# The row scatters of layer 0 set apart in a kernel of one scan and two expert layers

## The chip, the cores and the metric

The kernel runs on one core of a Trainium2 chip. The metric is the device time in microseconds (us) of one execution. The five engines have instruction streams of their own and meet at semaphores: TensorE (PE in the rows) multiplies, ScalarE (ACT) and VectorE (DVE) work on tiles and empty PSUM, GpSimd (POOL) does small elementwise work and issues the indirect DMAs, and SyncE (SP) issues the other DMAs. Each engine takes its own instructions strictly in order.

## What is computed

```python
for t in range(S):                         # gated scan, B = 2, S = 5056, D = 256
    h = f[:, t] * h + (1 - f[:, t]) * x[:, t];  y[:, t] = h
# then twice, on N = 10112 rows, E = 8 experts, F = 1024:
idx = argmax(logits, 1)                    # layer 0: normalised rows, layer 1: x @ w_gate
for e in range(E):
    mask = idx == e
    out[mask] = gate[mask, None] * (relu(x[mask] @ w1[e]) @ w2[e])
```

Each row goes through one expert per layer. The second layer routes the rows that the first one gives.

## The kernel before

**Rows and tables.** Rows are sorted by expert in DRAM. The table `X[0]` takes the rows of the scan, and `X[1]` takes the rows that layer 0 gives. A row holds two fp16 halves (high and low part), its scale and its token number, 1032 bytes in all. A tile is 128 rows of one expert, read back from the table by a transposing DMA (`t_load`, L755). A result row is written to its sorted place by an indirect DMA that GpSimd issues, the *row scatter*: `p_put` (L638, tile `row`) writes rows of the scan to `X[0]`, and the end of `m_slot` (L948, tile `trow`) writes rows of layer 0 to `X[1]`. Each scatter writes 128 rows.

**Steps.** The main loop goes through 332 executed *steps*. In a step TensorE does the first product of one tile and one half of the hidden columns (`mm1`, 24 matmuls, L780) into a PSUM tile `hps`. ScalarE and VectorE then empty it into `hT` (`evac`, L788 and L187), and TensorE does the second product of the step three before (`mm2`, 12 matmuls, L802; `lag` is 3). All other work is hung on the steps by a table of offsets and priorities, `(step offset, priority)`. Within a step, work is emitted by rising priority. `mm1` has 5, `evac` 50, `mm2` 55. On TensorE, ScalarE, GpSimd and SyncE the order is kept as emitted from step 17 on (`man`); on VectorE a scheduler sets it.

**Pairs.** Two tiles of layer 0 make a *pair*. When the second half of a tile is done, its row sums are copied to `osum`, and `m_sq` (L825, ScalarE) writes squares into a new `trow` buffer. Then come scaling (`m_scale`: VectorE's `pi`, `tsc`, `us`; GpSimd's `lf`, `COPY trow`, `inv`), logits, the choice of the expert (`m_top`, with GpSimd's `tsh`), the exponential, the gate weight (`m_gat`, with GpSimd's `trow<-tse,lf`) and the place in the table (`m_slot`). Before the change `m_slot` ends with the two scatters of the pair, back to back. There are five `trow` buffers (pool `rp`). Thus `m_sq` of the fifth pair after this one must wait until both of this pair's scatters have landed.

**Three groups of layer 0.** The first 4 tiles (group 1) and the last 21 (group 2, `swap`) run all their first halves and then all their second halves; the 58 between them (group 0) run both halves in turn, so that a pair ends every fourth step. In group 2, whose second halves run in steps 145 to 165, a pair ends every second step. I call its pairs P0 to P10, the last of one tile. P0's second tile leaves `mm2` in step 149, and each next pair two steps later. For group 2 the table `mg` puts `m_slot` nine steps on, so P0's scatters belong to step 158 before the change, P1's to step 160, and so on. P5's first `m_sq` stands in step 160 and needs P0's `trow` buffer; P6's stands in step 162 and needs P1's; P10's stands in step 170 and needs P5's. A step with two transposes of a pair needs six PSUM buffers in two steps, and pool `pb` has six, so in this stretch `hps` of a step takes the buffer that `hps` of two steps before gave back.

**Row groups of the scan** are four tiles; their scatters stand in four steps one after the other, at priority 12 (`put`), in a step's early part. In the middle of the program a period is eight steps long, with four scatters of `row` and four of `trow`.

Of the kernel before, what the change touches and what calls it, by code (L numbers as in the profile page):

```python
# [11 lines left out]
I32 = mybir.dt.int32  # L12
U32 = mybir.dt.uint32
ACTF = mybir.ActivationFunctionType
# [32 lines left out]
 'alias': 8,  # L47
 'mans': 17,
 'xtn': 48,
 'md': {'turn': (3, 58),  # L50
        'logits': (8, 3),
        'top': (8, 51),
# [2 lines left out]
        'rank': (10, 46),  # L55
        'slot': (11, 13),
        'up': (12, 45),
        'done': (12, 57)},
 'hiv': (2,),
 'y1': 'V',  # L60
 'wg': (0, 0, 0, 0),
# [63 lines left out]
def scan_moe_moe_kernel(ctx, tc, xf, emb, cst, tmp, w1a, w2a, w1b, w2b, out, seq, cfg=CFG):  # L125
# [6 lines left out]
    CT = 2  # L132
# [9 lines left out]
    BOUND = DUM + P - 1  # L142
# [3 lines left out]
    inside = [False]  # L146
# [30 lines left out]
    X = [dr.tile([DUM + P, RW // 2], I32, name=f"X{m}") for m in range(2)]  # L177
# [5 lines left out]
    V, A, G, T, SP = nc.vector, nc.scalar, nc.gpsimd, nc.tensor, nc.sync  # L183

    def stt(eng, out, in0, s, in1, op0, op1, **kw):
        assert eng is V
        return eng.scalar_tensor_tensor(out=out, in0=in0, scalar=s, in1=in1, op0=op0, op1=op1, **kw)  # L187
# [15 lines left out]
    def ins_of(i):  # L203
        return getattr(i, "ins", i)

    def x_write(m, i, group="Xw"):
        i = ins_of(i)
        tc.declare_no_dep(i, group=f"Xw{m}", reason="disjoint rows")
        tc.declare_no_dep(i, group=f"Xr{m}", reason="disjoint rows")
        if xpad[m]:  # L210
            tc.declare_no_dep(i, group=f"Xp{m}", reason="disjoint rows")
        tc.add_to_no_dep_group(f"{group}{m}", i)
        xw[m].append(i)
        if group == "Xp":
            xpad[m].append(i)
# [128 lines left out]
    now = [0]  # L344
# [288 lines left out]
    def p_put(q, rows):  # L633
        p = pq[q]
        for i in rows:
            if i >= p["g"]:
                return
            x_write(0, G.indirect_dma_start(out=X[0], out_offset=IndirectOffsetOnAxis(ap=p["sl"][:, i, 0:1], axis=0),  # L638
                                            in_=p["row"][:, i, :].bitcast(I32), in_offset=None, bounds_check=BOUND,
                                            oob_is_err=False))  # L640
            yield


# [69 lines left out]


    ring = {}

    wreg = [T.alloc_register(f"wa{i}") for i in range(16)]
    vreg = [T.alloc_register(f"va{i}") for i in range(4)]
# [65 lines left out]
    def evac(t, h):  # L784
        hps = t.pop("hps")
        hT = hp.tile([P, 8, P], F16, name="hT", tag="hT", bufs=LAG + 2)
        hh = hT.rearrange("p (a c) q -> p a (c q)", a=2)
        A.activation(out=hh[:, 0], in_=hps, func=ACTF.Relu)  # L788
        stt(V, hh[:, 1], hps, 0.0, hh[:, 0], ALU.max, ALU.subtract)
        t["hT", h] = hT  # L790

# [142 lines left out]
    def m_slot(d):  # L934
        g = len(d["t"])
        pz = d["er"]
        assert ranked[1] == 1
        ranked[1] = 0
        tt(V, pz, RK[:, G4:G4 + g], d["oh"][:, 0:g], ALU.mult)
        yield  # L940
        slf = sm.tile([P, CT, 1], F32, name="tslf", tag="tslf")[:, 0:g]
        V.tensor_reduce(out=slf, in_=pz, axis=AX.X, op=ALU.add)
        yield
        sl = sm.tile([P, CT, 1], I32, name="tsl", tag="tsl")[:, 0:g]
        stt(V, sl, slf, 1.0, d["inv"].unsqueeze(2), ALU.mult, ALU.add)
        yield
        for i in range(len(d["t"])):
            x_write(1, G.indirect_dma_start(out=X[1], out_offset=IndirectOffsetOnAxis(ap=sl[:, i, 0:1], axis=0),  # L948
                                            in_=d["row"][:, i].bitcast(I32), in_offset=None, bounds_check=BOUND,
                                            oob_is_err=False))  # L950
            yield

    def m_up(d):
        rank_up(1, d["oh"], CT)
# [26 lines left out]
    for m in range(2):  # L981
        done = 0
# [13 lines left out]
        for part in (tl, tails[m]):  # L996
            for j in range(0, len(part), CT):
                d = dict(t=part[j:j + CT], at=j)
# [25 lines left out]
    def at(s, prio, fn, *a):  # L1024
        seqn[0] += 1
        slots.setdefault(s, []).append((prio, seqn[0], fn, a))
# [26 lines left out]
    for c in range(NCH):  # L1053
        b = s0[c]
        PO = cfg["p"]

        def pa(name, fn, arg, b=b):
            if c < cfg["cps"][0] // CT and name in cfg["urgent"]:
                fn = first_of_all(fn)
            at(b + PO[name][0], PO[name][1], fn, arg)  # L1060

        if 2 <= c < cfg["alias"]:
            at(first - 2 + (c - 2) // 2, 2, p_load, c)
        elif c >= 2:
            pa("load", p_load, c)
        for name, fn in (("gate", p_gate), ("scan", p_scan), ("mm", p_mm), ("sq", p_sq), ("pow", p_pow), ("hi", p_hi), ("lo", p_lo)):
            pa(name, fn, c)
        if c % 2 or c == NCH - 1:
            q = c // 2
            for name, fn in (("norm", p_norm), ("top", p_top), ("rank", p_rank), ("rec", p_rec), ("exp", p_exp), ("slot", p_slot),  # L1070
                             ("up", p_up), ("gat", p_gat)):
                pa(name, fn, q)
            b, prio = s0[c] + PO["put"][0], PO["put"][1]
            if b < 0:
                at(b, prio, first_of_all(p_put) if c < cfg["cps"][0] // CT else p_put, q, range(G4))
            else:
                for j in range(G4):
                    at(b + j, prio, p_put, q, (j,))

            def cp0(q):  # L1080
                for m, cnt, n, fin, key in cpl:
                    if m == 0 and key not in xcnt and cnt <= min(NT, (q + 1) * G4):
                        checkpoint(m, n, fin, key, min(NT, (q + 1) * G4))

            pa("cp", cp0, q)
# [104 lines left out]
    def fin_unit(u, i):  # L1190
        t, h = units[u]
        if t["grp"] and h == 0:
            new_acc(t)
            at(i + 1, 10, o_partial, t)
        elif h == 1:
            if t["m"] == 1:
                at(i + 1, 10, s2, t)
                return
            MO = dict(cfg["m"], **cfg["mg"]) if t["grp"] else dict(cfg["m"], **cfg["md"]) if by_dma(t["pair"]) else cfg["m"]

            def ma(name, fn, arg):
                at(i + MO[name][0], MO[name][1], fn, arg)

            ma("sum", o_sum, t)
            ma("sq", m_sq, t)
            d = t["pair"]
            if t["pi"] == len(d["t"]) - 1:
                for name, fn in (("scale", m_scale), ("split", m_split), ("turn", m_turn), ("turn2", m_turn2),
                                 ("logits", m_logits), ("top", m_top), ("exp", m_exp), ("rank", m_rank),
                                 ("gat", m_gat), ("slot", m_slot), ("up", m_up), ("done", done_pair)):  # L1210
                    ma(name, fn, d)

    def drain(g):
        for _ in g or ():
            pass
# [8 lines left out]
    def last_tiles(m):  # L1224
        tl = tails[m]
        if not tl:
            return
        n = counts[m]
        inside[0] = True
        if m:  # L1230
            with tc.If(n > tl[0]["j"], label=f"tail{m}"):
                us = [(t, h) for t in tl for h in range(2)]
                for i in range(len(us) + 2):
                    if i < len(us):
                        t, h = us[i]
                        if h == 0:
                            t_load(t, 0)
                            t_reg(t)
                        mm1(t, h)
                        evac(t, h)  # L1240
                    if i >= 2:
                        t, h = us[i - 2]
                        mm2(t, h, h == 0, h == 1)
                        if h == 1:
                            drain(s2(t))
            return
        with tc.If(n > tl[0]["j"], label=f"tail{m}"):
            kept[0] = {}
            assert ranked[1] == 0
            for d in [t["pair"] for t in tl if t["pi"] == 0]:  # L1250
                for t in d["t"]:
                    t_load(t, 0, qp.tile([P, 8, TW], F16, name="xt8", tag="q")[:, 0:4, 0:P])
                    t_reg(t)
                    for h in range(2):
                        mm1(t, h)
                        evac(t, h)
                        mm2(t, h, h == 0, h == 1)
                    drain(o_sum(t))
                    m_sq(t)
                for fn in (m_scale, m_split, m_turn, m_turn2, m_logits, m_top, m_exp, m_rank, m_gat, m_slot, m_up):  # L1260
                    drain(fn(d))
                routed[0] += len(d["t"])
            kept[0] = None
        inside[0] = False
# [4 lines left out]
    with ExitStack() as region:  # L1269
# [5 lines left out]
        i = first - 2  # L1275
# [117 lines left out]
```

## Time and profile before

| | |
|---|---|
| median of 3 runs | 1064.48 us (1055.07, 1064.48, 1067.7) |
| the profiled execution's own time | 1052.77 us |
| its span, first to last instruction | 1050.9 us |
| granted TensorE clock, mean | 0.985 |
| TensorE busy | 996.1 us (95%) |
| VectorE, ScalarE, GpSimd busy | 602.3, 529.2, 407.8 us |
| software DMA queue (the scatters) | 31.51 MB, 11.7% of 16 engines |
| TensorE's slices (tenths of 40 equal slices) | 5557 in the first four, then 9 |

Read it from TensorE. After the first four slices, in which the scan starts and the first tiles are routed, it is nearly always busy. A later step can lengthen the time only where TensorE is made to wait, or give time back only where it waits now. In a timeline row the first number is the start in us, the second the busy time, and the brackets hold the idle time of that engine just before and what ended it.

### The profile page before, as it was taken

Reading aid. Unit: us, or ns where it says so; the run is one execution under the profiler, and the core shown is the slowest. Engines: PE = TensorE matmul, PEld = TensorE weight load, DVE = VectorE, ACT = ScalarE, POOL = GpSimd, SP = SyncE. Lnnn points to the kernel's source line nnn. Section 1 sums busy time; section 2 is a strip of 40 time slices with the busy share of each in tenths; the row PEclk is TensorE's granted clock in tenths of the full one; section 3 lists DMA queues with packets and bytes.
Section 4 is the critical chain, followed back from the end, with each engine's and each line's share of the span. In section 5 each row is a group of like instructions: output and inputs, shape, how many; then the busy total and the mean of one; then the engine's idle time right before and its main releaser. Section 6 shows DMA issues by size and latency. Waiting matters only on the chain. (4 is left out here: it accounts for less than half of the span.)

```text
span 1050.9 us, 36737 instructions
## 1 busy us (share of the span) xinstructions
PE 996.1 (95%) x13267; PEld 932.6 (89%) x13267; DVE 602.3 (57%) x1927; ACT 529.2 (50%) x1301; POOL 407.8 (39%) x666
## 2 busy tenths in 40 slices
PE   5557999999999999999999999999999999999997
PEld 4436889999999999999998999999999999999997
DVE  7988877787778777665449778443222222222221
ACT  6978555665655565665346466443333333333332
POOL 5834645666666565332002550243222222222222
PEclk9967999999999999999999999999999999999999
DMA  9798436777677673875479699653322222222220
GB/s 352 244 342 209 132 59 120 144 136 130 124 127 127 152 125 94 195 196 149 62 170 205 123 197 267 117 103 72 52 52 53 52 53 48 45 50 44 47 51 31
DMA packets 195612, 132.69 MB, mean 126 GB/s; under 512 B 169601, under 2 KB 172558, under 8 KB 195440
## 3 DMA queue, kind: packets, MB, share of 16 engines
q1 hardware_dynamic: 172384, 60.18, 29.7%
q10 hardware_dynamic: 11200, 38.62, 14.7%
q0 software_dynamic: 11856, 31.51, 11.7%
q8 instruction: 118, 1.93, 0.8%
q14 instruction: 54, 0.44, 0.2%
HBM read 58.89 MB, written 38.85 MB: 93 GB/s over the span
## 5 line engine op out<-in xcount | busy, mean ns | idle before, releaser
L780 PE MATMUL hps<-xT,W 128*128 128x128 f16 x7968 | 504.9, 220 | 6.9 <-DVE hT L187 3.1
L802 PE MATMUL ops<-W,hT 128*128 x3984 | 489.3, 272 | 1.6 <-ACT acc L806 0.9
L780 PEld LDWEIGHTS <-W 128*128 x7968 | 475.6, 98 | 16.0 <-issue 6.3
L187 DVE SCALAR_TENSOR_TENSOR hT<-hps,hT 128x512 f16<-128x512 f32 x332 | 228.6, 688 | 318.4 <-ACT hT L788 315.7
L802 PEld LDWEIGHTS <-hT 128*128 128x128 f16 x3984 | 374.3, 98 | 41.4 <-issue 2.0
L788 ACT ACTIVATE hT<-hps 128x512 f16<-128x512 f32 x332 | 198.0, 596 | 303.2 <-PE hps L780 284.0
L970 POOL DMA_INDIRECT out<-osum,ti x83 | 81.1, 977 | 291.4 <-ACT osum L966 189.5
L948 POOL DMA_INDIRECT X<-trow,tsl x83 | 97.1, 1170 | 53.2 <-DVE tsl L187 18.0
L638 POOL DMA_INDIRECT X<-row,sl x79 | 92.8, 1174 | 55.1 <-issue 37.7
L966 ACT ACTIVATE osum<-ops,exr 128x256 f32<-128x256 f32 x62 | 29.3, 473 | 47.0 <-PE ops L802 44.8
L195 POOL TENSOR_TENSOR lf<-exr,us 128x2 f32<-128x2 f32 (+1 forms) x42 | 9.7, 231 | 102.6 <-DMA W<-WD 44.0
L187 DVE SCALAR_TENSOR_TENSOR W<-ws,W 128x1024 f16<-128x1024 f32 x34 | 41.5, 1220 | 8.7 <-ACT W L373 8.7
L373 ACT ACTIVATE W<-ws 128x1024 f16<-128x1024 f32 x35 | 37.1, 1060 | 12.5 <-DMA ws<-w2b 8.6
L825 ACT ACTIVATE trow<-osum 128x256 f16<-128x256 f32 x83 | 34.9, 420 | 16.0 <-DMA X<-trow,tsl 7.6
L492 DVE TENSOR_TENSOR_SCAN xf<-xf 128x256 f32<-128x256 f32 (+3 forms) x64 | 42.8, 710 | 0.1
L507 PE MATMUL yt<-cs,xf 128*128 128x128 f32 x126 | 28.3, 303 | 15.2 <-DVE xf L492 10.2
L814 ACT ACTIVATE osum<-ops 128x256 f32<-128x256 f32 x58 | 22.2, 382 | 38.3 <-PE ops L802 38.3
L187 DVE SCALAR_TENSOR_TENSOR trow<-osum,tsc,trow 128x256 f16<-128x256 f32 x83 | 36.7, 481 | 4.1 <-ACT trow L840 3.2
L187 DVE SCALAR_TENSOR_TENSOR xf<-xf 128x512 f32<-128x512 f32 (+1 forms) x32 | 21.8, 681 | 26.7 <-POOL xf L192 19.9
L547 ACT ACTIVATE row<-yt,sc 128x256 f16<-128x256 f32 x79 | 33.5, 481 | 6.5 <-DVE sc L192 6.5
L840 ACT ACTIVATE trow<-osum,tsc 128x256 f16<-128x256 f32 x62 | 28.1, 500 | 16.5 <-DVE tsc L192 14.9
L187 DVE SCALAR_TENSOR_TENSOR row<-yt,sc,row 128x256 f16<-128x256 f32 x79 | 36.0, 472 | 0.2 <-ACT row L547 0.2
(149 smaller groups left out, 929.2 us busy)
## 6 DMA issues: line engine op xcount, KB each, us to landing
xf<-xf ACTq DMA_DIRECT2D x28, 512.0 KB
ws<-w1b ACTq DMA_DIRECT2D x16, 512.0 KB
ws<-w2b ACTq DMA_DIRECT2D x16, 512.0 KB
W<-w1a SPq DMA_DIRECT2D x11, 512.0 KB
W<-xf SPq DMA_DIRECT2D x8, 512.0 KB
ws<-w2a ACTq DMA_DIRECT2D x8, 512.0 KB
WD<-wq SPq DMA_DIRECT2D x8, 512.0 KB
W<-WD SPq DMA_DIRECT2D x8, 512.0 KB
```

Of the source, the lines that this page charges most:

```text
L187: return eng.scalar_tensor_tensor(out=out, in0=in0, scalar=s, in1=in1, op0=op0, op1=op1, **kw)
L373: A.activation(out=hi, in_=src, func=ACTF.Copy, scale=64.0)
L492: V.tensor_tensor_scan(out=t[:, k, lo:hi], data0=t[:, 2 + k, lo:hi], data1=t[:, k, lo:hi], initial=init, op0=ALU.mult, op1=ALU.subtract)
L547: A.activation(out=p["row"][:, o + i, 0:D], in_=yv(d["yt"][i]), func=ACTF.Copy, scale=p["sc"][:, o + i:o + i + 1])
L638: x_write(0, G.indirect_dma_start(out=X[0], out_offset=IndirectOffsetOnAxis(ap=p["sl"][:, i, 0:1], axis=0), in_=p["row"][:, i, :].bitcast( ...
L780: T.matmul(out=hps[:, c, :], lhsT=w, rhs=xt[:, a, :], start=(n == 0), stop=(n == 5))
L788: A.activation(out=hh[:, 0], in_=hps, func=ACTF.Relu)
L802: T.matmul(out=o, lhsT=hT[:, a + k, :], rhs=w[:, b * D:(b + 1) * D], start=(first and k == 0 and n == 0), stop=(last and k == 3 and n == 2))
L825: A.activation(out=d["row"][:, i, D:2 * D], in_=t["O"], func=ACTF.Square, scale=0.25, accum_out=d["ss"][:, i:i + 1])
L948: x_write(1, G.indirect_dma_start(out=X[1], out_offset=IndirectOffsetOnAxis(ap=sl[:, i, 0:1], axis=0), in_=d["row"][:, i].bitcast(I32), in ...
L966: A.activation(out=r, in_=o, func=ACTF.Copy, scale=ex0[:, 0:1])
L970: i = ins_of(G.indirect_dma_start(out=out, out_offset=IndirectOffsetOnAxis(ap=ti, axis=0), in_=r, in_offset=None, bounds_check=N - 1, oob_ ...
```

## The change

The two scatters of a pair leave `m_slot` and become two calls of a new function `m_put`. The first stands in the step in which `m_slot` ended before; the second stands two steps later in group 0 and one step later in groups 1 and 2 (`'apart': (2, 1)`). Their priority is 40 where `m_slot` has a low one (groups 1 and 2, and the pairs of group 0 that are turned by DMA), and 55 otherwise. From step 17 on the row scatters of the scan move from priority 12 to 54 of the same step (`'late'`). Every scatter after step 17 gets one more wait: for the last ScalarE `evac` that had been recorded when it was emitted. At priority 40 that is the `evac` of the step in front, at 54 and 55 that of its own step. `done` of the DMA-turned pairs, which counts routed tiles, moves from 12 to 13 steps. No instruction is added or removed.

```diff
+ 'apart': (2, 1),
+ 'late': 54,
...
-        'done': (12, 57)},
+        'done': (13, 57)},
...
-            x_write(0, G.indirect_dma_start(out=X[0], out_offset=IndirectOffsetOnAxis(ap=p["sl"][:, i, 0:1], axis=0),
+            x_write(0, paced(G.indirect_dma_start(out=X[0], out_offset=IndirectOffsetOnAxis(ap=p["sl"][:, i, 0:1], axis=0),
...
+    evs = []
+
+    def paced(i):
+        if now[0] > cfg["mans"] and not inside[0]:
+            tc.add_manual_dep(ins_of(i), evs[-1].name, mybir.DependencyInfo(mybir.DependencyClass.Sync, mybir.DependencyReason.DATA),
+                              reason="one step apart")
+        return i
...
-        A.activation(out=hh[:, 0], in_=hps, func=ACTF.Relu)
+        evs.append(ins_of(A.activation(out=hh[:, 0], in_=hps, func=ACTF.Relu)))
...
-        yield
-        for i in range(len(d["t"])):
-            x_write(1, G.indirect_dma_start(out=X[1], out_offset=IndirectOffsetOnAxis(ap=sl[:, i, 0:1], axis=0),
-                                            in_=d["row"][:, i].bitcast(I32), in_offset=None, bounds_check=BOUND,
-                                            oob_is_err=False))
-            yield
+        d["sl"] = sl
+
+    def m_put(d, i):
+        if i < len(d["t"]):
+            x_write(1, paced(G.indirect_dma_start(out=X[1], out_offset=IndirectOffsetOnAxis(ap=d["sl"][:, i, 0:1], axis=0),
...
-                    at(b + j, prio, p_put, q, (j,))
+                    at(b + j, prio if b < cfg["mans"] else cfg["late"], p_put, q, (j,))
...
+                for j in range(CT):
+                    at(i + MO["slot"][0] + cfg["apart"][bool(t["grp"])] * j, 40 if MO["slot"][1] < 40 else 55, m_put, d, j)
```

The order of instructions on TensorE, ScalarE and SyncE stays as it was. GpSimd's order changes in two ways. The first place is a period in the middle of the program (group 0). `X_100<-trow,tsl` is a scatter of a pair, `X_99<-row,sl` one of the scan's rows, `xf` a gate of the scan, `tsh` and `lf` small products of layer 0. Before:

```order
L192 TENSOR_SCALAR xf<-xf,fa,fb 128x256 x2
L948 DMA X_100<-trow,tsl 82048x258 x2
L638 DMA X_99<-row,sl 82048x258
L195 TENSOR_TENSOR tsh<-tsh,lf 128x16
L638 DMA X_99<-row,sl 82048x258
L195 TENSOR_TENSOR lf<-exr,us 128x2
```

and with the change, at the same place on GpSimd:

```order
L194 TENSOR_SCALAR xf<-xf,fa,fb 128x256 x2
L959 DMA X_100<-trow,tsl 82048x258
L640 DMA X_99<-row,sl 82048x258 x2
L197 TENSOR_TENSOR tsh<-tsh,lf 128x16
L959 DMA X_100<-trow,tsl 82048x258
L640 DMA X_99<-row,sl 82048x258
L197 TENSOR_TENSOR lf<-exr,us 128x2
```

The pair's second scatter has gone behind `tsh`, and one row scatter that stood ahead of the first rows shown now stands behind the pair's first scatter.

The second place is group 2, where a pair ends every second step. Before, on GpSimd, from the scaling of one pair (`lf`, `COPY`, `inv`) to the scatters of the pair four ahead of it:

```order
L195 TENSOR_TENSOR lf<-exr,us 128x2
L844 COPY trow<-exr 128x2
L192 TENSOR_SCALAR inv<-exr 128x2
L195 TENSOR_TENSOR tsh<-tsh,lf 128x16
L195 TENSOR_TENSOR trow<-tse,lf 128x2
L948 DMA X_100<-trow,tsl 82048x258 x2
```

and with the change, from the first scatter of one pair to the first of the next:

```order
L959 DMA X_100<-trow,tsl 82048x258
L197 TENSOR_TENSOR lf<-exr,us 128x2
L853 COPY trow<-exr 128x2
L194 TENSOR_SCALAR inv<-exr 128x2
L197 TENSOR_TENSOR tsh<-tsh,lf 128x16
L959 DMA X_100<-trow,tsl 82048x258
L197 TENSOR_TENSOR trow<-tse,lf 128x2
L959 DMA X_100<-trow,tsl 82048x258
```

The second scatter of a pair (the second DMA row) now stands behind `lf`, `COPY`, `inv` and `tsh` of the step after; `lf` belongs to the scaling of the pair four later. On VectorE some 25 small instructions around step 160 change places among themselves; elsewhere its order is the same but for two swaps of neighbours.

## Rows read from the trace of the kernel before

**Rows 1.** The page's 40 slices: tenths busy, for TensorE.

```profile
PE   5557999999999999999999999999999999999997
```

**Rows 2.** Busy time by stretch; the first line names the columns.

```profile
core 0: us, PE busy (x) PEld busy (x) DVE busy (x) ACT busy (x) POOL busy (x), PEclk, DMA share, GB/s
...
300.00:325.00 25.00, 25.00 (x352) 23.84 (x350) 20.34 (x88) 15.22 (x47) 15.96 (x27) 1.00 0.75 129
...
575.00:600.00 25.00, 22.79 (x334) 21.23 (x332) 18.91 (x91) 12.79 (x37) 12.32 (x27) 1.00 0.72 128
```

**Rows 3.** Waits of TensorE from 150 us on: us in total, times, longest.

```profile
PE hps L780 <- DVE osum L195: 1.9, 1, 1.9
```

**Rows 4.** GpSimd's timeline in group 0: start, busy, line, out<-in, idle before.

```profile
300.86 1.46 POOL L948 DMA_INDIRECT X<-trow,tsl  x1 [0.16 <-POOL xf L192]
302.63 1.23 POOL L948 DMA_INDIRECT X<-trow,tsl  x1 [0.31 <-issue]
304.16 0.97 POOL L638 DMA_INDIRECT X<-row,sl  x1 [0.30 <-issue]
...
306.10 1.01 POOL L638 DMA_INDIRECT X<-row,sl  x1 [0.51 <-issue]
308.37 0.18 POOL L195 TENSOR_TENSOR lf<-exr,us 128x2 f32<-128x2 f32 x1 [1.26 <-DVE tse L187]
```

**Rows 5.** ScalarE's timeline in the same stretch, two of the `evac`.

```profile
302.79 0.60 ACT L788 ACTIVATE hT<-hps 128x512 f16<-128x512 f32 x1 [1.13 <-PE hps L780]
...
305.49 0.60 ACT L788 ACTIVATE hT<-hps 128x512 f16<-128x512 f32 x1 [0.96 <-PE hps L780]
```

**Rows 6.** GpSimd's timeline in group 2, P0 to P5.

```profile
571.89 0.97 POOL L948 DMA_INDIRECT X<-trow,tsl  x1 [0.30 <-issue]
...
576.22 0.21 POOL L195 TENSOR_TENSOR tsh<-tsh,lf 128x16 f32<-128x16 f32 x1
...
578.87 1.51 POOL L948 DMA_INDIRECT X<-trow,tsl  x1 [0.30 <-issue]
584.69 0.37 POOL L195 TENSOR_TENSOR lf<-exr,us 128x2 f32<-128x2 f32 x1 [4.31 <-DVE tsh L187]
...
585.92 0.30 POOL L195 TENSOR_TENSOR tsh<-tsh,lf 128x16 f32<-128x16 f32 x1
...
589.42 0.97 POOL L948 DMA_INDIRECT X<-trow,tsl  x1 [0.30 <-issue]
...
605.83 0.97 POOL L948 DMA_INDIRECT X<-trow,tsl  x1 [0.30 <-issue]
```

**Rows 7.** ScalarE's timeline in group 2: first `m_sq` of P5, P6, P7, P10.

```profile
582.12 0.42 ACT L825 ACTIVATE trow<-osum 128x256 f16<-128x256 f32 x1 [3.84 <-DMA X<-trow,tsl]
...
587.20 0.42 ACT L825 ACTIVATE trow<-osum 128x256 f16<-128x256 f32 x1 [2.13 <-DVE toh L187]
...
593.83 0.42 ACT L825 ACTIVATE trow<-osum 128x256 f16<-128x256 f32 x1 [2.87 <-DMA X<-trow,tsl]
...
610.72 0.42 ACT L825 ACTIVATE trow<-osum 128x256 f16<-128x256 f32 x1 [0.94 <-DMA X<-trow,tsl]
```

**Rows 8.** TensorE's timeline: `mm1` of steps 162, 170 and 172.

```profile
584.36 1.50 PE L780 MATMUL hps<-xT,W 128*128 128x128 f16 x24
...
609.20 1.50 PE L780 MATMUL hps<-xT,W 128*128 128x128 f16 x24
...
615.25 1.50 PE L780 MATMUL hps<-xT,W 128*128 128x128 f16 x24
```

**Rows 9.** VectorE's timeline: its part of `evac` of steps 160 and 170.

```profile
583.14 0.69 DVE L187 SCALAR_TENSOR_TENSOR hT<-hps,hT 128x512 f16<-128x512 f32 x1 [2.92 <-ACT hT L788]
...
612.59 0.68 DVE L187 SCALAR_TENSOR_TENSOR hT<-hps,hT 128x512 f16<-128x512 f32 x1
```

**Rows 10.** Line L948, the pairs' scatters, over the run: from issue to landing.

```profile
DMA to landing us min/median/max: 2.6/4.6/6.1
```

More of the change, by code (lines that the diff above doesn't have):

```diff
@@ L637, in p_put @@
                 return
-            x_write(0, G.indirect_dma_start(out=X[0], out_offset=IndirectOffsetOnAxis(ap=p["sl"][:, i, 0:1], axis=0),
-                                            in_=p["row"][:, i, :].bitcast(I32), in_offset=None, bounds_check=BOUND,
-                                            oob_is_err=False))
+            x_write(0, paced(G.indirect_dma_start(out=X[0], out_offset=IndirectOffsetOnAxis(ap=p["sl"][:, i, 0:1], axis=0),
+                                                  in_=p["row"][:, i, :].bitcast(I32), in_offset=None, bounds_check=BOUND,
+                                                  oob_is_err=False)))
             yield
@@ L945, in m_slot @@
         stt(V, sl, slf, 1.0, d["inv"].unsqueeze(2), ALU.mult, ALU.add)
-        yield
-        for i in range(len(d["t"])):
-            x_write(1, G.indirect_dma_start(out=X[1], out_offset=IndirectOffsetOnAxis(ap=sl[:, i, 0:1], axis=0),
-                                            in_=d["row"][:, i].bitcast(I32), in_offset=None, bounds_check=BOUND,
-                                            oob_is_err=False))
-            yield
+        d["sl"] = sl
+    def m_put(d, i):
+        if i < len(d["t"]):
+            x_write(1, paced(G.indirect_dma_start(out=X[1], out_offset=IndirectOffsetOnAxis(ap=d["sl"][:, i, 0:1], axis=0),
+                                                  in_=d["row"][:, i].bitcast(I32), in_offset=None, bounds_check=BOUND,
+                                                  oob_is_err=False)))
     def m_up(d):
@@ L1261, in last_tiles @@
                     drain(fn(d))
+                for j in range(CT):
+                    m_put(d, j)
                 routed[0] += len(d["t"])
```

## Prediction

> **What bounds the kernel now.** I read the page's slices first, then the busy times by stretch, then TensorE's waits, then the timelines of GpSimd, ScalarE, VectorE and TensorE where the scatters stand.
>
> The slices show TensorE at nine tenths or more from the fifth slice on [rows 1]. The change acts from step 17 on, which lies behind the four slow slices, so it cannot touch the start. From 300 to 325 us TensorE is busy for all 25.00 us while GpSimd has work for 15.96 us [rows 2]. A scatter that lands sooner is worth nothing there, since nothing on TensorE waits for it. The one stretch with real idle time is 575 to 600 us, with 22.79 of 25 us busy [rows 2], and the longest wait of TensorE after 150 us lies in it: 1.9 us [rows 3]. That stretch is group 2, where pairs end every second step. So the question is what the change does to group 2, and whether it disturbs group 0.
>
> What the reader should see in group 2 is one chain. ScalarE's `m_sq` of P5 begins at 582.12 after 3.84 us of idle time that ended with the landing of a `trow` scatter [rows 7]. The buffer it needs is P0's, and P0's second scatter was issued at 571.89 [rows 6]. P7 waits 2.87 us in the same way for P2 (issue 589.42, start 593.83), and P10 waits 0.94 us for P5 (605.83, 610.72) [rows 6, 7]. The second scatter of a pair is thus already the last event ahead of ScalarE in this stretch, and everything later on ScalarE, `evac` above all, stands behind it. VectorE's `evac` of step 160 waits 2.92 us for ScalarE [rows 9], and `mm1` of step 162 starts at 584.36, 0.53 us after that `evac` ended (583.14 + 0.69) [rows 8, 9]. The buffers of the accumulator leave about half a microsecond between the two.
>
> **The change part by part.** *Row scatters at priority 54, and the waits in group 0.* Laid out from the rows: the pair's first scatter can start at 300.86 as now and ends at 302.3. Two row scatters follow. The first needs an `evac` that is over. The second needs the one that ends at 303.39 (302.79 + 0.60), and GpSimd comes to it at about 303.6. `tsh` follows, then the pair's second scatter, then a row scatter behind the `evac` that ends at 306.09, where GpSimd comes at about 307. With 1.0 us for that one, `lf` starts at about 308.4, and it starts at 308.37 now, after 1.26 us of idle time for a result of VectorE [rows 4, 5]. The new waits fall where GpSimd was not ready anyway, so I cost them at nothing. The cover is GpSimd's free time, 25 − 15.96 = 9.0 us in 25 [rows 2]; if each of the seven or so scatters of a period really waited 1.3 us, the cover would be gone. That is the fourth case below. What stands behind the waiting scatters on GpSimd is the gate of the scan, `ri`, `lf` and `tsh`; TensorE needs what comes of them steps later.
>
> *The second scatter two steps later in group 0.* The buffer is needed again by the fifth pair after it, 20 steps on, while the pair's scatters stand 8 to 13 steps after the pair. It costs nothing. `done` at 13 has the same answer: the checkpoint for layer 1 is set off by pairs whose offsets don't change.
>
> *The second scatter one step later in group 2.* Here the order on GpSimd counts. P0's second scatter now stands behind `lf`, `COPY`, `inv` and `tsh` of step 159. Today that `tsh` ends at 576.43 (576.22 + 0.21) [rows 6]. With the 0.30 us that stands ahead of a scatter [rows 6], the issue moves from 571.89 to about 576.7. When does it land? The nearest issue is P1's second at 578.87, for which P6 was released by 587.20, at most 8.3 us later [rows 6, 7]. With 8.3 us P5 is released at 585.0 rather than 582.12, 2.9 us late. The bounds are 582.1 (it lands no later than now, since other traffic held up the early issue) and 576.7 + 10.2 = 586.9 (the 571.89 to 582.12 of today).
>
> *And then a loop closes.* `lf` in front of P1's second scatter is the scaling of P5 and so needs P5's `m_sq`. P1's scatter now waits for P5, P6 waits for P1's scatter, P2's scatter waits for P6, and so on to P10. Before the change both scatters of P1 stood ahead of P5's scaling, so there was no such loop of two steps. Its length comes from rows of today. From `m_sq` of P5 (582.12) to the end of `tsh` (585.92 + 0.30 = 586.22) and 0.30 us to the issue is 4.4 us [rows 6, 7]. Then the scatter must land. The least on the page is 2.6 us and the middle 4.6 [rows 10]; P7's and P10's waits give 4.4 (589.42 to 593.83) and 4.9 (605.83 to 610.72) [rows 6, 7], but for the second of two scatters issued back to back, and the new one goes alone. I take 3.6, halfway from 2.6 to 4.6, with 2.6 and 4.9 as bounds. The loop is then 8.0 us (7.0 to 9.3), while TensorE needs 6.05 for the same two steps (609.20 to 615.25) [rows 8].
>
> *The sum.* There are five loops from P5 to P10. P10's `m_sq` would start at 585.0 + 5 × 8.0 = 625.0 and not at 610.72 [rows 7], 14.3 us late. TensorE can take up some of it: `mm1` of step 172 starts 2.0 us after the `evac` of step 170 has ended (615.25 against 612.59 + 0.68) [rows 8, 9]. It loses 14.3 − 2.0 = 12.3 us. With the low bounds it is 582.1 + 35.0 = 617.1, so 6.4 − 2.0 = 4.4 us; with the high ones 586.9 + 46.5 = 633.4, so 20.7 us. After step 172 the pairs are over and TensorE sets the pace again, with nothing given back. Against the profiled execution's own 1052.77 us the sum is 1065.
>
> For the landing there is a rule to weigh. The rows have waits of 4.4 and 4.9 us and a least of 2.6 [rows 6, 7, 10]. The Trainium skill, "DMA: Bandwidth & Descriptors", section "Anatomy of one DMA — SWDGE (gpsimd) path", gives a transfer issued by GpSimd a fixed 2.0 us and its bytes at 436 GB/s. As an estimate from that page, 132 KB would take 2.3 us, the loop 6.7, and the loss would be 5.8 rather than 12.3 us. No row has a landing that short, so the measurement decides.
>
> **How this stands to the median.** The profiled execution is the fastest of the four shown (1052.77; 1055.07, 1064.48, 1067.7). The rows don't tell where the others spent up to 15 us more. Their mean is 1060.0. The loss of 12 us comes on top of any of them, so I set it on the mean: 1072 us.
>
> **The rivals.** *One: nothing is seen.* `m_sq` comes no later because the late scatters, alone in their queue, land so fast that the loop keeps TensorE's 6.05 us. It would take a landing of 1.65 us (6.05 − 4.4), below the least on the page, or a shorter way from `m_sq` to the issue: VectorE's new order around step 160 does put some work into its idle 2.92 us [rows 9]. The time would be that of before, 1060 within 4.
>
> *Two: faster.* Transposes and scatters share the DMA engines. If P0's and P1's four scatters in a burst are what made TensorE wait around 575 us, pulling them apart gives that back. The 575 to 600 us stretch holds 2.2 us of idle time [rows 2]; if the slower executions lose their 2 to 15 us to bursts too, those come back as well, and all runs lie at 1050 to 1053. It decides from the point where P5 is released earlier than 582.1 although its scatter was issued 4.8 us later. Against it stands that TensorE waits for nothing in group 0, where the bursts are the same.
>
> *Three: slower by much more.* The waits for `evac` hold GpSimd up in group 0 after all, `tsh` and `ri` come late to VectorE, and VectorE's `evac` with them. If each of the twelve periods between steps 24 and 120 lost 2 us of TensorE, it would be 24 us on top of the loop's 12: 1096. It decides when the waits of a period add to more than GpSimd's 9.0 free us. The layout above speaks against it.
>
> **How the numbers follow.** The loop in group 2: 0.58. Nothing seen: 0.23. Faster: 0.10. Much slower: 0.09. The likeliest gives 1072, by itself 1064 to 1081 on the mean (the bounds 4.4 and 20.7). The range takes in the larger part of the no-change case below and the slower executions above: 1056 to 1088, which leaves out most of the faster case and of the much slower one. A measurement of this kernel tells about 2%, 21 us, from no change. A loss of 12 us is 1.2% and stays within it. Slower by over 2% needs the upper end of the loop on a slow set of runs, or the third rival: 0.14. Faster by over 2% would need more than the profile has to give: 0.03. The rest, 0.83, is within 2%.
>
> **What would show each step.** In the changed kernel the second scatter of P0 should start near 576.7, behind `tsh`, and ScalarE's idle time ahead of `m_sq` of P6 to P10 should end with the landing of `X<-trow,tsl` at a spacing of some 8 us. TensorE should show idle time ahead of `hps` in steps 162 to 172 and none that is new from 175 to 430 us. In group 0 `lf` and `ri` should keep their places in the step. The prediction is wrong if P6 to P10 follow at 6 us or less, if TensorE gains idle time in group 0, or if the stretch from 575 to 600 us loses the idle time it has.

## The result, and the profile after

The kernel with the change takes 1068.17 us (median of 22 executions, 1060.78 to 1075.95), the kernel before 1063.65 us (22 executions, 1055.07 to 1070.58). The ratio is 1.0055, with a 95% interval of 1.0032 to 1.0079: 5.9 us slower (3.4 to 8.4). A second comparison of the same two, made beside f2, f4 and f7 below, gave 1.0102 (1.0069 to 1.0134), 10.8 us. Both together, weighted by their intervals, put the loss near 7.5 us. Forecast were 1072 us and a loss of 12: the direction held, the time lies in the range, and the size was too large. The range takes in the case of no change too, so the traces say more here than the number.

The profiled execution of the changed kernel took 1061.07 us with a span of 1059.3. Its line numbers are 2 to 12 higher than before (`m_sq` is L834, the pairs' scatter L959, `mm1` L789). Busy time by stretch, after [rows 2], and under it the last stretch for the kernel before:

```profile
core 0: us, PE busy (x) PEld busy (x) DVE busy (x) ACT busy (x) POOL busy (x), PEclk, DMA share, GB/s
300.00:325.00 25.00, 25.00 (x354) 23.84 (x352) 19.84 (x84) 14.52 (x46) 15.50 (x28) 1.00 0.83 129
575.00:600.00 25.00, 22.52 (x325) 20.63 (x324) 16.60 (x75) 10.95 (x32) 11.86 (x22) 1.00 0.53 120
600.00:625.00 25.00, 22.10 (x322) 20.11 (x320) 17.48 (x90) 12.19 (x35) 13.03 (x26) 1.00 0.45 120
```

```profile
600.00:625.00 25.00, 25.00 (x383) 23.89 (x381) 20.80 (x93) 15.63 (x35) 14.79 (x28) 1.00 0.86 192
```

In the middle of the program TensorE is as full as before. In group 2 it now loses 2.5 and 2.9 us in two stretches; before, it lost 2.2 in the first and nothing in the second. What ScalarE waits for says why. This is the page's line of `m_sq`, before and after: the count and busy time, then the idle time ahead of it and what ended most of that.

```profile
L825 ACT ACTIVATE trow<-osum 128x256 f16<-128x256 f32 x83 | 34.9, 420 | 16.0 <-DMA X<-trow,tsl 7.6
```

```profile
L834 ACT ACTIVATE trow<-osum 128x256 f16<-128x256 f32 x83 | 35.1, 423 | 26.7 <-DMA X<-trow,tsl 20.3
```

The waits for the landing of a pair's scatter went from 7.6 to 20.3 us; P8's wait of 4.12 us, which the profile puts down to `issue`, is not in that sum. ScalarE's timeline has them, at the first `m_sq` of P5, P6, P7 and P10 [rows 7]:

```profile
584.77 0.42 ACT L834 ACTIVATE trow<-osum 128x256 f16<-128x256 f32 x1 [3.94 <-DMA X<-trow,tsl]
...
591.75 0.42 ACT L834 ACTIVATE trow<-osum 128x256 f16<-128x256 f32 x1 [4.03 <-DMA X<-trow,tsl]
...
598.98 0.42 ACT L834 ACTIVATE trow<-osum 128x256 f16<-128x256 f32 x1 [4.27 <-DMA X<-trow,tsl]
...
620.29 0.42 ACT L834 ACTIVATE trow<-osum 128x256 f16<-128x256 f32 x1 [4.06 <-DMA X<-trow,tsl]
```

And GpSimd's, from P5's scaling to the second scatters of P1, P2 and P5 [rows 6]:

```profile
587.11 0.36 POOL L197 TENSOR_TENSOR lf<-exr,us 128x2 f32<-128x2 f32 x1 [3.50 <-DVE tse L939]
...
588.33 0.22 POOL L197 TENSOR_TENSOR tsh<-tsh,lf 128x16 f32<-128x16 f32 x1
588.70 1.39 POOL L959 DMA_INDIRECT X<-trow,tsl  x1 [0.15 <-issue]
...
596.11 1.07 POOL L959 DMA_INDIRECT X<-trow,tsl  x1 [0.16 <-issue]
...
617.35 1.07 POOL L959 DMA_INDIRECT X<-trow,tsl  x1 [0.16 <-issue]
```

Read one turn of the loop across the two: P5's `m_sq` at 584.77, P1's second scatter issued at 588.70 (3.93 us on), P6's `m_sq` at 591.75 (3.05 us on). Five turns take 620.29 − 584.77 = 35.52 us, 7.1 us each. Before, the same five pairs took 610.72 − 582.12 = 28.60 [rows 7]. `mm1` of step 172 starts at 623.25, 8.0 us later than before [rows 8], and only 0.43 us behind VectorE's `evac` of step 170 (622.14 + 0.68) [rows 9]. Of these 8.0 us, 1.8 are older than the loop: `mm1` of step 160 starts at 579.91, before at 578.10. The other 6.2 came with the loop. In f1, a second profile of the changed kernel, step 172 is 10.6 us late, 1.4 of them at step 160, so 9.2 came with the loop. The two rows of the profile after:

```profile
623.25 1.50 PE L789 MATMUL hps<-xT,W 128*128 128x128 f16 x24 [1.10 <-DVE ter L189]
```

```profile
622.14 0.68 DVE L189 SCALAR_TENSOR_TENSOR hT<-hps,hT 128x512 f16<-128x512 f32 x1
```

TensorE's waits from 150 us on show the same; the largest was 1.9 us for `osum` before [rows 3]:

```profile
PE hps L789 <- DVE ter L189: 2.4, 2, 1.3
PE RK L438 <- DVE ter L197: 1.7, 4, 0.5
```

### The profile page after: what moved, and what is told of

It is laid out like the page before. It is cut to its first block, busy times and chain, and to the rows that moved or that the text cites. A ratio compares the mean times of both kernels' runs of the same rounds, so it can differ in the third digit from the quotient of the medians.

```text
span 1059.3 us, 36772 instructions
## 1 busy us (share of the span) xinstructions
PE 995.9 (94%) x13267; PEld 932.2 (88%) x13267; DVE 601.8 (57%) x1927; ACT 526.8 (50%) x1301; POOL 407.7 (38%) x666
## 3 DMA queue, kind: packets, MB, share of 16 engines
q10 hardware_dynamic: 11200, 38.62, 13.8%
## 5 line engine op out<-in xcount | busy, mean ns | idle before, releaser
L789 PE MATMUL hps<-xT,W 128*128 128x128 f16 x7968 | 506.0, 220 | 9.3 <-DVE hT L189 3.1
L789 PEld LDWEIGHTS <-W 128*128 x7968 | 475.6, 98 | 19.9 <-issue 9.6
L959 POOL DMA_INDIRECT X<-trow,tsl x83 | 95.6, 1152 | 52.8 <-DVE hT L189 16.4
L640 POOL DMA_INDIRECT X<-row,sl x79 | 89.7, 1136 | 54.5 <-PE ops L811 16.6
L834 ACT ACTIVATE trow<-osum 128x256 f16<-128x256 f32 x83 | 35.1, 423 | 26.7 <-DMA X<-trow,tsl 20.3
```

The source lines that it names most:

```text
L640: x_write(0, paced(G.indirect_dma_start(out=X[0], out_offset=IndirectOffsetOnAxis(ap=p["sl"][:, i, 0:1], axis=0), in_=p["row"][:, i, :].bi ...
L789: T.matmul(out=hps[:, c, :], lhsT=w, rhs=xt[:, a, :], start=(n == 0), stop=(n == 5))
L834: A.activation(out=d["row"][:, i, D:2 * D], in_=t["O"], func=ACTF.Square, scale=0.25, accum_out=d["ss"][:, i:i + 1])
L959: x_write(1, paced(G.indirect_dma_start(out=X[1], out_offset=IndirectOffsetOnAxis(ap=d["sl"][:, i, 0:1], axis=0), in_=d["row"][:, i].bitca ...
```

## The experiments

The theory (A) is the loop: P1's second scatter stands behind P5's scaling, which needs P5's `m_sq`, and P6's `m_sq` needs P1's buffer. The rivals are the added waits or the late row scatters that hold GpSimd up (B), and another mix of transfers (C). The loop in the table is a fifth of the time from P5's first `m_sq` to P10's; the next column is ScalarE's idle time for `X<-trow,tsl` ahead of `m_sq`. TensorE's own pace is 6.05 us. Each time stands against executions of the kernel before made beside it. Their medians were 1063.65 us for the first row of the changed kernel, 1060.4 for e1, e2, e3 and e6, 1053.5 for e4, e7 and e8, 1056.5 for f1, f2, f4 and f7, and 1060.8 for g8.

| kernel | loop, us | ScalarE's wait, us | against before, us (95%) |
|---|---|---|---|
| before | 5.72 | 7.6 | |
| changed | 7.10 | 20.3 | +5.9 (3.4 to 8.4) |
| changed, again (f1) | 7.39 | 28.0 | +10.8 (7.3 to 14.2) |
| e1 same step | 6.10 | under 0.5 | −0.1 (−3.3 to 3.0) |
| e6 one step later, ahead of the scaling | 6.11 | 0 | +0.6 (−2.4 to 3.6) |
| e2, f2 group 2's part alone | 7.09, 7.37 | 22.7, 27.7 | +9.1 (5.7 to 12.4), +10.5 (6.6 to 14.5) |
| e4, f4 without the added wait | 7.35, 7.08 | 27.8, 26.3 | +13.8 (12.0 to 15.7), +8.2 (5.1 to 11.5) |
| e7, f7 both scatters behind | 8.14, 8.32 | 33.5, 32.6 | +14.2 (12.3 to 16.2), +13.3 (9.8 to 16.9) |
| e3 changed, six buffers | 6.06 | 0 | −0.8 (−3.5 to 1.8) |
| e8 before, six buffers | 6.22 | 0 | +0.4 (−2.7 to 3.7) |
| g8 both behind, six buffers | 6.43 | 3.1 | +2.1 (−1.3 to 5.5) |

**e1: the delay of groups 1 and 2 taken back.**

```diff
- 'apart': (2, 1),
+ 'apart': (2, 0),
```

> The changed kernel, but in groups 1 and 2 both scatters of a pair stand in the same step again; late row scatters, two steps in group 0 and all added waits stay. Theory A (loop: a pair's second scatter stands behind the scaling of the pair five later, whose buffer the next pair's scatter must free): P6 to P10 of `m_sq` follow at about 6 us and not at 7.1, some 6 us come back, time +0 to +3 us on the kernel before. Theory B (the added waits for `evac` or the late row scatters hold GpSimd up): nothing comes back, +6 us stay. Theory C (scatters set apart land in another mix of transfers and delay transposes): between, the change in group 0 keeps its share.

All of it came back. The added waits, the late row scatters and the two steps of group 0 are all still there, so together they cost nothing that can be measured, and they gain nothing that can be measured either.

**e2: group 2's part alone, on the kernel before.** `m_slot` issues the first scatter as it did; in groups 1 and 2 the second is hung on the next step.

```diff
+        d["sl"] = sl
         for i in range(len(d["t"])):
+            if d["t"][0]["grp"] and i and not inside[0]:
+                return
...
+                if t["grp"]:
+                    at(i + MO["slot"][0] + 1, 40, m_put, d, 1)
```

> The kernel before, with one thing of the change: in groups 1 and 2 the second scatter of a pair stands one step later, behind the scaling that belongs to that step. No added wait, row scatters and group 0 as before. Theory A: the whole loop is there, `m_sq` of P6 to P10 at 7.0 to 7.3 us, +6 us on the kernel before. Theory B: no wait is added, +0 to +1 us. Theory C: +6 us less the share of group 0, about +4.

The loop is there with 7.09 us, and the whole loss with it. Theory B falls: no wait was added here and no row scatter moved. ScalarE's line in this kernel:

```profile
L825 ACT ACTIVATE trow<-osum 128x256 f16<-128x256 f32 x83 | 35.0, 421 | 29.9 <-DMA X<-trow,tsl 22.7 <-issue 3.9 <-DVE osum L195 2.3
```

**e3: six buffers.**

```diff
-    rp = Pool(ctx.enter_context(tc.tile_pool(name="rp", bufs=5)))
+    rp = Pool(ctx.enter_context(tc.tile_pool(name="rp", bufs=6)))
```

> The changed kernel with six `trow` and `row` buffers in place of five; nothing else is edited. Theory A: the sixth pair and not the fifth waits for a pair's scatters, so the loop spans four steps (7.1 us against 12.1 us that TensorE needs) and no longer binds: ScalarE's waits for the landing of `X<-trow,tsl` fall from 20 us to near nothing, the time is +0 to +3 us on the kernel before, and less if the waits of the kernel before for the same buffers (7.6 us of ScalarE) cost it something too. Theory B and theory C: the buffers are not what is short, +5 to +7 us stay.

The order on TensorE, ScalarE, GpSimd and SyncE is that of the changed kernel, and the second scatter is still issued a step behind the first (P0's at 573.56 and 578.67). Only the buffer is free earlier, and the loss is gone. With that theory C falls, which would have left 5 to 7 us:

```profile
L834 ACT ACTIVATE trow<-osum 128x256 f16<-128x256 f32 x83 | 35.0, 422 | 2.3 <-DVE ct L681 1.2 <-DVE osum L197 1.1
```

**e6: one step later, but ahead of the scaling.**

```diff
-                    at(i + MO["slot"][0] + cfg["apart"][bool(t["grp"])] * j, 40 if MO["slot"][1] < 40 else 55, m_put, d, j)
+                    at(i + MO["slot"][0] + cfg["apart"][bool(t["grp"])] * j, (20 if t["grp"] and j else 40) if MO["slot"][1] < 40 else 55, m_put, d, j)
```

> The changed kernel; in groups 1 and 2 the second scatter still belongs to the step after the first's and still waits for its `evac`, but stands ahead of `lf`, `COPY` and `inv` of that step. Theory A (it is the place behind the scaling that closes the loop): the issue needs only the `evac` that follows `m_sq`, about 1.5 us instead of 4, the loop is about 4.5 us and slack, `m_sq` of P6 to P10 follow at about 6 us, time +0 to +3 us. If the delay of a step or the wait for `evac` by itself costs (theory B), +5 to +7 us stay.

On GpSimd this puts the second scatter right behind the first again, ahead of `lf`, `COPY`, `inv` and `tsh`, with the wait for the later `evac` kept. In the trace the second scatters of P0 to P5 start 1.4 us behind the first, as before the change, so the kept wait holds nothing up. The loss is gone. It was the place behind the scaling that cost time; what the wait costs inside the loop is the question of e4.

**e4 and f4: the added wait taken away.** The order is kept.

```diff
-        if now[0] > cfg["mans"] and not inside[0]:
+        if False:
```

> The changed kernel without the added wait of a scatter for `evac`; the order on every engine is that of the changed kernel, row for row. Theory A (the loop goes through `lf`, `COPY`, `inv` and `tsh`, which stand ahead of the scatter on GpSimd): P6 to P10 of `m_sq` still follow at 7.0 to 7.3 us, +5 to +7 us on the kernel before. Theory D (the scatter of P1 in the loop waits for the `evac` that stands behind P5's `m_sq` on ScalarE, and that wait closes the loop): spacing near 6 us, +0 to +2 us.

> The changed kernel without the added wait, beside the changed kernel. The first look put it at +14 us on another chip, with 8 us of that in the eight steps behind the loop where TensorE waited for transposes. If the wait keeps scatters and transposes apart and so saves time, it is slower than the changed kernel by 5 us or more here too. If that was chance, it stands within 3 us of the changed kernel.

The loop is the same (7.35 and 7.08 us), so theory D falls. The size of e4, +13.8, was a miss. In its trace 8.2 us more than in the profile of before lie behind the loop, in steps 183 to 190, where TensorE waited for transposes. Beside the changed kernel (f1, +10.8) the same kernel stood at +8.2, so nothing shows that the wait saves or costs time. e4's waits of TensorE from 640 to 690 us:

```profile
PE hps L789 <- DMA xT<-X: 5.6, 2, 3.4
PE hps L789 <- DVE hT L189: 1.0, 1, 1.0
```

**e7 and f7: a larger dose.**

```diff
-                    at(i + MO["slot"][0] + cfg["apart"][bool(t["grp"])] * j, 40 if MO["slot"][1] < 40 else 55, m_put, d, j)
+                    at(i + MO["slot"][0] + (1 if t["grp"] else cfg["apart"][0] * j), 40 if MO["slot"][1] < 40 else 55, m_put, d, j)
```

> The changed kernel with a larger dose: in groups 1 and 2 the first scatter of a pair goes one step later too, so that both stand back to back behind `lf`, `COPY`, `inv` and `tsh` of that step, the second some 1.3 us behind the first. Theory A: the loop gets longer by those 1.3 us, 8.4 us if the second lands as fast as the lone scatter of the changed kernel does (2.6 to 3.0 us), 9.0 to 9.8 us if it lands in the 4.4 to 4.9 us of the kernel before, where two went back to back. P10's `m_sq` would then be late by 2.65 + 1.3 + 5 x (8.4 - 5.72) = 17 us (up to 24), less the 2 us that TensorE takes up: +15 us on the kernel before (up to +22). Theory E (the loss is one of a second scatter that lies apart, by its mix with other transfers): pairs are together again, about +0 to +3 us.

> Both scatters of a pair one step later in groups 1 and 2, beside the changed kernel: its loop was 8.1 us in the first trace against 7.1. Five loops with 1 us more and a first release 1 to 4 us later: 6 to 9 us slower than the changed kernel on the same chip.

The loop grew from 7.1 to 8.14 and 8.32 us, and the time with it; theory E falls, since the two scatters stand together here. One turn in e7, from ScalarE's and GpSimd's timelines:

```profile
597.54 0.42 ACT L834 ACTIVATE trow<-osum 128x256 f16<-128x256 f32 x1 [4.97 <-DMA X<-trow,tsl]
...
605.38 0.42 ACT L834 ACTIVATE trow<-osum 128x256 f16<-128x256 f32 x1 [4.89 <-DMA X<-trow,tsl]
```

```profile
601.30 1.07 POOL L959 DMA_INDIRECT X<-trow,tsl  x1 [0.15 <-issue]
602.68 0.97 POOL L959 DMA_INDIRECT X<-trow,tsl  x1 [0.30 <-DVE tmx L905]
```

P6's `m_sq` at 597.54, the second scatter at 602.68 (5.14 us on), P7's `m_sq` 2.70 us behind that. e7 met its expectation. f7 didn't: it stood only 2.5 us above f1 (13.3 − 10.8), not 6 to 9. Part of that is f1, one of whose five turns took 9.04 us. From P5 to P10, f7's trace is 4.65 us longer than f1's (41.61 and 36.96). Where the other 2 us went isn't settled.

**g8: the larger dose with six buffers.** The edit of e7 and that of e3.

> Both scatters of a pair one step later in groups 1 and 2, with six `trow` and `row` buffers in place of five; the order on TensorE, ScalarE, GpSimd and SyncE is that of the kernel with both scatters behind, row for row. Theory A (the loss is the chain through the reuse of a buffer and nothing else): with the sixth buffer the chain spans four steps (8.2 us against 12.1) and all of the +13 to +14 us goes: 0 to +3 us on the kernel before, `m_sq` of P5 to P10 at 6.0 to 6.3 us. If the late scatters cost something by another way as well (their transfers, GpSimd's order), +4 us or more stays.

Of 14 us, 2 are left, with an interval of −1.3 to 5.5. It takes in none, but also the 4 us that were to mark a second way. The loop is down to 6.43 us, a little above the 6.0 to 6.3 expected; a wait of 3.1 us for a scatter is left. The chain through the reuse of a buffer is thus the cause of the loss in the changed kernel (e3), and of most of it at least in the larger dose.

**e8: the kernel before with six buffers.** The edit of e3, on the kernel before.

> The kernel before with six `trow` and `row` buffers in place of five. Theory A says that the kernel before is already at the edge of the same loop: ScalarE's 7.6 us of waits for the landing of `X<-trow,tsl` go away, and the idle 2.2 us of TensorE between 575 and 600 us go with them as far as they come from the buffers and not from late transposes: -1 to -2.5 us on the kernel before. If transposes made that idle time, +0 us.

ScalarE's 7.6 us of waits went, and the time stayed. They had cost nothing that can be measured; the interval (−2.7 to 3.7) doesn't rule out the 1 to 2.5 us expected. No kernel here is faster than the one before by more than its interval.

**f1, f2: the changed kernel and group 2's part, side by side.** f1 is the changed kernel as it is, f2 the kernel of e2.

> The changed kernel itself, beside the three that follow, all on one chip. Its first comparison gave +5.9 us (3.4 to 8.4) where the loop of the single trace accounts for 6 to 7. Expected again: +5 to +9 us on the kernel before.

> The kernel before with the second scatter one step later in groups 1 and 2 and nothing else, beside the changed kernel. If the added waits, the late row scatters and the two steps of group 0 are worth nothing, it stands within 3 us of the changed kernel. If they give something back, it is slower than the changed kernel by more than that (the first look put it at +9 against +6).

f1's +10.8 lies above the 5 to 9 us expected, which its interval (7.3 to 14.2) reaches. In its trace P0's scatter took 7.54 us to release P5 and P4's 4.69 to release P9, where the profile after has 4.49 and 2.58. Group 2's part alone (+10.5) makes up the whole change (+10.8); nothing of the rest shows.

## Why the prediction was right, and where it was off

**The mechanism held.** The new wait, its place and its owner were those named: ScalarE's `m_sq` of P6 to P10 behind the second scatter of P1 to P5, which stands behind the scaling of the pair before. e2 makes it alone. e1 and e6 break it by putting the second scatter ahead of the scaling again, e3 by a sixth buffer with the late scatter left where it is, and each gives the loss back.

**The loop was mis-sized.** It was put at 8.0 us, as 4.4 from `m_sq` to the issue and 3.6 to land. In the profile after, the five turns have 3.93, 4.36, 4.36, 4.35 and 4.36 to the issue (mean 4.27), and 3.05, 2.87, 2.72, 2.58 and 2.94 from there to `m_sq` (mean 2.83). In f1 the second term has a mean of 3.13, with four of 2.6 to 2.9 and one of 4.69. So the landing was the term that was off, by 0.5 to 0.8 us. Over five turns the loop's 0.6 to 0.9 us make 3 to 4.5 us, and 12.3 less that is 8 to 9, against 5.9 and 10.8 measured. The rows of before with 4.4 and 4.9 us were no guide, nor was the profile's middle of 4.6 us. The 4.4 holds the late part told of in the last section, and the 4.9 stands at a DMA share of 0.75. I took both waits for what the second of two scatters in a row costs, but in e7, where two go in a row as well, the second released the next pair after 2.64, 2.70 and 2.24 us in the first three of the five turns, and after 3.27 and 3.69 in the last two. The estimate from the Trainium skill, "DMA: Bandwidth & Descriptors", section "Anatomy of one DMA — SWDGE (gpsimd) path", was 2.3 us for the landing. The quiet turns, at 2.6 to 3.1, lie between it and my 3.6, nearer to it. The loss of 5.8 us that it gave is near the 5.9 of the first comparison, but in part by chance, since it holds 2.9 us for the first release, too much for this execution; the second comparison lies above.

**P5's start was right by chance.** It was put at 585.0 and was 584.77. But the steps ahead of it, from 155 on, already ran 2.9 to 3.8 us late in this execution, and step 160 itself 1.8. P0's second scatter went out at 580.28, not at 576.7, and took 4.49 us to release P5, not 8.3: two errors that cancel. Against its own step P5 was only 0.84 us late, not 2.9 (in f1 2.36). With 0.84 for the first release, 6.92 for five turns (35.52 − 28.60) and 1.57 taken up (next), the trace's sum is 6.19, the 6.2 us that came with the loop.

**What TensorE takes up** was put at 2.0 us. P10's `m_sq` was 9.57 us late and `mm1` of step 172 8.0, so it took up 1.6. The prediction had read the 0.53 us between VectorE's `evac` of step 160 and `mm1` of step 162 as the room that the PSUM buffers leave. There they don't tie the two: in the profile after that `mm1` starts at 586.12, while the `evac` still runs (585.80 + 0.69). From step 164 on they do (593.90 behind 592.78 + 0.69), and the term was nearly right.

**Group 0 at nothing** held, by e1 and by f2. In the profile after, GpSimd's rows of a period [rows 4] and two `evac` [rows 5] are these:

```profile
301.49 1.47 POOL L959 DMA_INDIRECT X<-trow,tsl  x1 [0.17 <-POOL xf L194]
303.26 1.21 POOL L640 DMA_INDIRECT X<-row,sl  x1 [0.30 <-issue]
304.78 0.97 POOL L640 DMA_INDIRECT X<-row,sl  x1 [0.30 <-issue]
...
306.71 1.01 POOL L959 DMA_INDIRECT X<-trow,tsl  x1 [0.51 <-issue]
308.03 0.97 POOL L640 DMA_INDIRECT X<-row,sl  x1 [0.30 <-ACT row L526]
309.11 0.19 POOL L197 TENSOR_TENSOR lf<-exr,us 128x2 f32<-128x2 f32 x1
```

```profile
303.13 0.60 ACT L797 ACTIVATE hT<-hps 128x512 f16<-128x512 f32 x1 [1.05 <-PE hps L789]
...
306.37 0.60 ACT L797 ACTIVATE hT<-hps 128x512 f16<-128x512 f32 x1 [1.49 <-PE yt L511]
```

The first `evac` runs 0.34 us later than before, as all steps do there, and `lf` starts 0.74 us later: the new order and its waits took 0.4 us from GpSimd, which had 9.5 us free in 25. The statement that no idle time of TensorE would be new from 175 to 430 us was wrong for this one execution: it lost 1.1 us from 395 to 430 us. That isn't the change. The first row is the profile after, the second f1, the same kernel in another execution, the third e2, with the kernel before in this stretch:

```profile
395.00:430.00 35.00, 33.88 (x484) 31.81 (x482) 23.29 (x105) 16.16 (x44) 19.49 (x35) 1.00 0.48 119
```

```profile
395.00:430.00 35.00, 35.00 (x515) 33.35 (x513) 24.68 (x118) 17.46 (x46) 20.13 (x35) 1.00 0.56 127
```

```profile
395.00:430.00 35.00, 32.72 (x463) 30.30 (x462) 22.38 (x106) 16.06 (x44) 16.96 (x28) 1.00 0.49 109
```

**The rivals.** *Nothing seen* needed a landing of 1.65 us; none in these turns was under 2.2. *Faster* needed bursts that cost TensorE time; e3 sets the scatters of group 2 apart without the loop and e1 those of group 0, and neither gains anything that can be measured. *Much slower* needed GpSimd's free time used up; it lost 0.4 us in a period.

**The base.** The loss was set on 1060.0, the mean of four executions. The 22 of the first comparison have a median of 1063.65. That error of 3.7 us went the other way, so the forecast time is nearer to the result than the forecast loss.

## What to carry to other kernels

When an instruction is moved later on an in-order engine, look at what it is now queued behind, and whether that needs, through a buffer, what the moved instruction frees: a chain of that kind sets a pace of its own, and costs its excess over the bound engine once per turn. Count the buffers between the two ends: here five closed the loop, and six or a place four small instructions earlier opened it. An idle time that ends with a landing is no loss by itself: e8 removed 7.6 us of it and gained nothing that could be measured.

## What the runs showed of the hardware

**A row scatter lands in 2.2 to 3.1 us where the DMA engines have room, right behind another scatter too, and in up to 10.2 us where they don't; some land late with room.** The 10.2 us are those of P0's scatter before (571.89 to 582.12), at a DMA share of 1.25. Each row is the stretch from an issue to the `m_sq` that it released; its length is the second number, and the last three are the granted clock, the DMA share and GB/s. The share adds up the time of all packets over 16 engines, so it can pass 1. The changed kernel, P2's and P5's scatter:

```profile
596.11:598.98 2.87, 2.87 (x40) 2.65 (x40) 1.39 (x6) 0.00 (x0) 2.27 (x3) 1.00 0.37 95
617.35:620.29 2.94, 2.93 (x41) 2.73 (x41) 0.79 (x3) 0.00 (x0) 1.28 (x2) 1.00 0.42 109
```

f1, P0's and P4's:

```profile
578.36:585.90 7.54, 6.19 (x92) 5.86 (x93) 3.59 (x11) 1.06 (x1) 3.32 (x3) 1.00 1.25 245
...
610.96:615.65 4.69, 4.68 (x60) 4.18 (x59) 1.39 (x6) 0.00 (x1) 2.27 (x3) 1.00 0.36 91
```

e7, the second of two in a row, P0's and P2's:

```profile
583.70:589.61 5.91, 5.29 (x78) 4.91 (x75) 1.65 (x7) 0.00 (x0) 1.66 (x2) 1.00 1.01 195
602.68:605.38 2.70, 2.70 (x45) 2.61 (x43) 0.93 (x5) 0.00 (x0) 1.18 (x2) 1.00 0.20 68
```

And before, P2's and P5's:

```profile
589.40:593.80 4.40, 4.40 (x65) 4.12 (x63) 3.68 (x19) 1.56 (x3) 2.92 (x7) 1.00 0.29 75
605.80:610.70 4.90, 4.90 (x81) 4.73 (x79) 3.67 (x21) 1.96 (x4) 2.92 (x7) 1.00 0.75 133
```

The long landings at shares of 0.75 to 1.25 go with the load. Those of 4.40 and 4.69 us at 0.29 and 0.36 are of another kind. A scatter's semaphore counts 16 parts. In the trace's records 15 parts of these two had landed by 592.51 and 613.41, and the last came at 593.73 and 615.54. In each stretch the profile has one packet of the queue that it names `instruction`; the first row is the kernel before, the second f1:

```profile
q8 instruction: 1, 0.02, 1.7%
```

```profile
q8 instruction: 1, 0.02, 2.1%
```

By the records this packet of 16 KB ran from 591.26 to 592.45 and from 612.84 to 614.38, and one packet of the scatter started just as it ended, at 592.44 and 614.37. The late scatters of P4 in f2 and e4 (4.30 and 4.07 us) show the same. In f4 and e2 the packet of instructions started at the end of P4's transfer, and these landed in 2.72 and 2.63 us. So a fetch of instructions that holds up one part in 16 fits every one of these; no run moved such a fetch, and it is not shown as the cause. All of this is read off the traces; no run changed the load by itself.

**The clock.** A gap can cost more than itself. In e7 TensorE stood idle for 3.14 us ahead of a product for the logits at 592.13. The granted clock is 0.84 from 590 to 595 us and 0.82 in the next 5 us, a mix of the two levels (1.2 and 2.4 GHz). `mm1` took 2.48 us in it and 1.50 behind it:

```profile
592.13 0.21 PE L893 MATMUL lp<-wg,x 128*128 128x16 f16 x2 [3.14 <-ACT x L885]
...
594.78 2.48 PE L789 MATMUL hps<-xT,W 128*128 128x128 f16 x24
598.91 1.50 PE L789 MATMUL hps<-xT,W 128*128 128x128 f16 x24
```

In neither profile of the changed kernel did a stretch of 5 us between 571 and 625 us have a clock below 1.00; e2's had 0.89 and 0.77 from 585 to 595 us.

**What varies between executions** isn't explained by the change. From 395 to 430 us TensorE lost between 0 and 2.3 us, with no releaser that the trace shows. At the head of layer 1 (steps 183 to 190) its waits for `xT` were none in the profile of before, 0.4 us after, 2.0 in f1, 4.3 in e6, 5.6 in e4 and 6.0 in g8. The weight fetches of 512 KB, the zero rows and the transposes meet there; which of them comes late was not tried.
